# Retention opening in four steps of four heads by 256 tokens, in place of four chunks of eight heads by 128 tokens

## The chip, the cores and the metric

The kernel runs on one core of a Trainium2 chip. The core has a matrix engine (TensorE, "PE" in the profile, with its weight loads as "PEld"), VectorE (DVE), ScalarE (ACT), GpSimd (POOL) and SyncE (SP), which here only issues transfers. Each engine takes its own instructions in order and waits on semaphores for the others. Sixteen DMA engines move data between the chip's memory (HBM) and the on-chip SBUF; TensorE writes its results into PSUM, which has eight banks of 2 KB in each of 128 partitions. The metric is the device time of one execution in microseconds, the median of several.

## The reference

Two layers follow one another. The first is retention over q, k, v of 8 batches, 8 heads, 576 positions and 64 numbers each: causal attention without softmax, with a decay for each head. The second is a bilinear feed-forward network (FFN) over the 4608 tokens, 512 wide with 1536 features.

```python
scores = scale * np.matmul(q, k.transpose(0, 1, 3, 2))
gamma = 1.0 - 2.0 ** (-5.0 - np.arange(H))
rel = pos[:, None] - pos[None, :]
Dmat = np.where(rel >= 0, gamma[:, None, None] ** rel, 0.0)
attn_out = np.matmul(scores * Dmat, v)
x = attn_out.transpose(0, 2, 1, 3).reshape(B * S, H * D)
return ((x @ w_a) * (x @ w_b)) @ w_out
```

Since the decay is a power of the distance, `gamma**(s-t) = gamma**s * gamma**-t`. The kernel scales v by `gamma**-t` (the table `vs`), masks the plain scores, and scales the result by `scale * gamma**s` (the table `qs`). What keys of earlier chunks contribute is carried in a state, the sum of k^T v for each head.

## The kernel before

**The FFN** (`ffn_block`, L581 to L641) goes in blocks of 512 tokens (two of 256 after the first). A block forms `pa = x w_a` (L592) and `pb = x w_b` (L607) for each of 12 groups of 128 features, 4 matmuls each, casts pa on ACT (L600), multiplies on DVE (L612) and then forms `po` (L627), which leaves through `osb`. It reads x transposed, the tile `xT` of four chunks of 128 features. The first block takes its feature groups in runs of 3, 4 and 5, pa first and then pb (`WCOLS`, L579), since the weights arrive in these pieces.

**The retention** is woven into the FFN's instruction stream on PE, at places written by hand as PE cost (`todo`, L718 to L740). Most of it is done in pairs of 128-token chunks by `stretch`, with the PE array split into four quarters of 64x64 (`QUADS`). Only the first six chunks of 128 tokens are done one by one, and the first four of these form the opening: they have to be ready before the FFN can begin with its first 512 tokens.

**The opening** is the loop at L663 to L679. For a chunk i of 128 tokens with all 8 heads:
- `load(i)` (L116) brings q, k and v, 256 KB each, by SP (L121). A row of the transfer is one token of one head, 64 float32, 256 bytes.
- `cast(i)` (L241): q to bf16 on ACT (L250), k on DVE for chunks 0 and 3 (L252) and on POOL for chunks 1 and 2 (L254), v times `vs` on POOL (L255).
- `transposes(i)` (L262): four PE transposes for q and four for k (L269), each group into a PSUM tile `tp`; ACT copies q's out, DVE k's (L272).
- `scores(i)` (L307): eight matmuls `sc` of 64 rows (L316), one for each head, keys by queries; DVE masks them into `sT` in two instructions (L322).
- `state(i)` (L275): four matmuls `kv` (L287) add a chunk to the running sum in one PSUM bank that stays in place through the batch; ACT casts the diagonal blocks to the state (L304, L305).
- `outputs(i)` (L330): eight matmuls from the state (L341, none for chunk 0) and eight from the keys (L349) give `o`; DVE scales it by `qs` into xT (L356).

The program order of the loop sets each engine's queue. Before chunk i's state is cast, ACT has the q cast of chunk i+1 in front of it; `flush` puts the masks on DVE. The `warm` matmuls (L647) are products of the identity with itself, without use for the result; `idle` (L656) gives their number ahead of the scores and behind the state. The tiles `tp`, `kv2`, `w`, `pa`, `pb` and `po` share a ring of four PSUM banks (`ps_ffn`), `sc` has two banks, `kv` and `o` one each.

POOL also issues the weight transfers, which cast to bf16 on the way: `load_w(0, W1)` and `load_w(W1, W2)` ahead of the cast of chunk 3, the rest and `wo` after the loop. SP then waits with a small transfer (`gate`, L685) for the first of `wo` before it issues the loads of chunks 4, 5 and later pairs.

Ahead of the loop POOL makes index tables, the identity and the masks, ACT the tables `vs` (L184) and the first 640 columns of `qs` (L191); the remaining 128 columns of `qs` and the tables of the pairs (`pair_tables`, L198) are made during the first FFN block.

Of the kernel before, what the change touches and what calls it, by code (L numbers as in the profile page):

```python
# [10 lines left out]
FP32 = mybir.dt.float32  # L11
# [7 lines left out]
def kernel(  # L19
# [10 lines left out]
    nc = tc.nc  # L30
# [28 lines left out]
    def pool(name, bufs, space=None):  # L59
# [18 lines left out]
    opening = ExitStack()  # L78
    ps_open = opening.enter_context(
        tc.tile_pool(name="ps_open", bufs=1, space=PS))  # L80
    ps_o = {}
# [61 lines left out]
    for i in range(4):  # L143
        load(i)


    idxp_i = const.tile([128, PER], INT32)
    nc.gpsimd.iota(idxp_i[:, 0:MID + 1], pattern=[[128, MID + 1]], base=0,
                   channel_multiplier=1)
    nc.gpsimd.iota(idxp_i[:, MID + 1:PER], pattern=[[128, PER - MID - 1]],  # L150
                   base=64, channel_multiplier=1)
    idxv_i = const.tile([128, BL, 2], INT32)
    nc.gpsimd.iota(idxv_i, pattern=[[256, BL], [128, 2]], base=0,
                   channel_multiplier=1)
# [6 lines left out]
    make_identity(nc, identity)  # L161
    mask = const.tile([128, 128], BF16)
    nc.gpsimd.memset(mask, 1.0)
    nc.gpsimd.affine_select(
        out=mask, in_=mask, compare_op=ALU.is_ge, fill=0.0,
        base=0, pattern=[[1, 128]], channel_multiplier=-1)
    mask2 = const.tile([128, 128], BF16)
    nc.gpsimd.tensor_copy(mask2, mask)
    nc.gpsimd.memset(mask2[0:64, 64:128], 0.0)
    mask3 = const.tile([128, 64], BF16)  # L170

    lgp = const.tile([128, HP], FP32)
    for c in range(HP):
# [4 lines left out]
    idxp_f = const.tile([128, PER], FP32)  # L178
    nc.vector.tensor_copy(idxp_f, idxp_i)
    nc.vector.tensor_scalar_add(idxp_f[64:128, MID:MID + 1],  # L180
                                idxp_f[64:128, MID:MID + 1], -float(S))
    vs = const.tile([128, PER, H], FP32)
    for h in range(H):
        nc.scalar.activation(vs[:, :, h], idxp_f, AF.Exp,  # L184
                             bias=0.0, scale=-math.log(gammas[h]))
# [12 lines left out]
    def pair_tables(step):  # L198
# [12 lines left out]
        else:  # L211
            make_qs(step - 5, S + 64, S + 192)
# [4 lines left out]
    for t in states:  # L217
        nc.vector.memset(t, 0.0)
# [10 lines left out]
    natural, transposed, kv_of, state_of, scored = {}, {}, {}, {}, {}  # L229
    sums_of, states_of = {}, {}  # L230
# [6 lines left out]
    def flush():  # L237
        while later:
            later.pop(0)()

    def cast(i, on="pool"):  # L241
# [11 lines left out]
        else:  # L253
# [4 lines left out]
            vs[:, i % PER, :].unsqueeze(2).to_broadcast([128, H, D]),  # L258
# [16 lines left out]
    def state(i):  # L275
# [5 lines left out]
        if not kv_of:  # L281
            kv_of[0] = ps_open.tile([128, HP, 128], FP32, tag="kv",
# [500 lines left out]
```

## Time and profile before

| | us |
|---|---|
| median of 4 runs (336.4 to 338.75) | 336.59 |
| the profiled execution, device time | 336.15 |
| its span, first to last instruction | 334.4 |
| PE busy in it | 321.6 (96%) |
| DVE / ACT / POOL busy | 164.6 / 124.6 / 112.3 |
| first pa matmul of the FFN starts at | 21.24 |

The span is divided into 40 slices of 8.4 us in the profile's rows of digits; a 9 means that the engine was busy for 90% of the slice or more. In the timeline a row has start, length, engine, source line, operation, output and input tiles with shapes, and, in brackets, how long the engine had been idle and what ended that. In the chain of waits a row has start, length and the work that the end depended on. In the stages a row has the stretch in us, its length, then busy time and instruction count of PE, PEld, DVE, ACT and POOL, the granted clock, the DMA share (over 1 where packets of one engine overlap) and GB/s. A PE matmul is pipelined: the length in its row includes a latency of some 0.2 to 0.3 us, while the next one may start after 0.03 to 0.2 us.

### The profile page before, as it was taken

Reading aid. Unit: us, or ns where it says so; the run is one execution under the profiler, and the core shown is the slowest. Engines: PE = TensorE matmul, PEld = TensorE weight load, DVE = VectorE, ACT = ScalarE, POOL = GpSimd, SP = SyncE. Lnnn points to the kernel's source line nnn. Section 1 sums busy time; section 2 is a strip of 40 time slices with the busy share of each in tenths; the row PEclk is TensorE's granted clock in tenths of the full one; section 3 lists DMA queues with packets and bytes.
Section 4 is the critical chain, followed back from the end, with each engine's and each line's share of the span. In section 5 each row is a group of like instructions: output and inputs, shape, how many; then the busy total and the mean of one; then the engine's idle time right before and its main releaser. Section 6 shows DMA issues by size and latency. Waiting matters only on the chain.

```text
span 334.4 us, 8313 instructions
## 1 busy us (share of the span) xinstructions
PE 321.6 (96%) x3458; PEld 165.4 (49%) x3458; DVE 164.6 (49%) x307; ACT 124.6 (37%) x261; POOL 112.3 (34%) x139
## 2 busy tenths in 40 slices
PE   2989999999999999999999999999999999999995
PEld 1544445857744454545454545454545454444443
DVE  4646346465746465476237623762475347414321
ACT  8534433443624343353225322523352334213321
POOL 4670016961547448266143603370330000000000
PEclk9999999999999999999999999999999999999999
DMA  9999999999999999999599259964960420020002
GB/s 172 207 187 208 210 199 211 263 210 204 164 195 233 185 216 255 191 189 172 142 228 191 59 144 194 185 113 134 217 92 3 127 63 2 3 94 31 0 33 94
DMA packets 152230, 50.35 MB, mean 151 GB/s; under 512 B 142848, under 2 KB 147712, under 8 KB 152192
## 3 DMA queue, kind: packets, MB, share of 16 engines
q1 hardware_dynamic: 147440, 45.10, 70.2%
q0 software_dynamic: 4752, 4.72, 8.8%
q8 instruction: 27, 0.44, 0.6%
q14 instruction: 11, 0.09, 0.1%
HBM read 37.75 MB, written 9.44 MB: 141 GB/s over the span
## 4 chain that ended last, share of the span: by engine, by line
PE 93%; DVE 2%; DMA 2%; SPq 1%; ACT 1%; issue 0%; POOL 0%; ACTq 0%; DVEq 0%
PE pa L592 28%; PE pb L607 28%; PE po L627 28%; DMA kf<-in_k_dram 2%; PE o L525 2%; PE o L538 1%; PE sc L499 1%; PE kv L448 1%; PE w L651 1%; PE tp L269 1%; SPq L121 1%; DVE sT L322 1%; PE sc L316 1%; PE o L349 0%; PE o L341 0%
## 5 line engine op out<-in xcount | busy, mean ns | idle before, releaser
L612 DVE TENSOR_TENSOR hT<-ha,pb 128x512 bf16<-128x512 bf16 (+1 forms) x120 | 75.8, 633 | 98.3 <-PE pb L607 86.7
L592 PE MATMUL pa<-xT,wa_sb 128*128 128x512 bf16 (+1 forms) x480 | 111.5, 358 | 1.3 <-DVE xT L356 1.1
L600 ACT CAST ha<-pa 128x512 bf16<-128x512 f32 (+1 forms) x120 | 64.9, 542 | 126.5 <-PE pa L592 125.9
L607 PE MATMUL pb<-xT,wb_sb 128*128 128x512 bf16 (+1 forms) x480 | 111.4, 358 | 0.1
L627 PE MATMUL po<-wo_sb,hT 128*128 128x512 bf16 (+1 forms) x444 | 97.3, 373 | 0.0
L607 PEld LDWEIGHTS <-wb_sb 128*128 128x128 bf16 x480 | 46.9, 98 | 47.7 <-issue 1.1
L592 PEld LDWEIGHTS <-wa_sb 128*128 128x128 bf16 x480 | 45.9, 98 | 47.7 <-issue 2.4
L627 PEld LDWEIGHTS <-hT 128*128 128x128 bf16 x444 | 42.4, 98 | 47.0
L388 POOL CAST qkb<-qf 64x1024 bf16<-64x1024 f32 x15 | 15.4, 1029 | 81.5 <-DMA qf<-in_q_dram 68.9
L638 DVE COPY osb<-po 128x512 f32<-128x512 f32 (+1 forms) x18 | 12.2, 676 | 42.9 <-PE po L627 42.9
L393 POOL TENSOR_TENSOR vb<-vf,vs 128x1024 bf16<-128x1024 f32 x15 | 28.5, 1901 | 7.7 <-DMA vf<-in_v_dram 2.8
L636 ACT COPY osb<-po 128x512 f32<-128x512 f32 (+1 forms) x19 | 10.9, 574 | 49.0 <-PE po L627 49.0
L547 DVE TENSOR_TENSOR xT<-o,qs 128x512 bf16<-128x512 f32 x30 | 19.6, 681 | 5.5 <-PE o L538 5.5
L467 DVE TENSOR_TENSOR sums<-kv,sums 128x256 f32<-128x256 f32 x47 | 19.8, 422 | 4.6 <-PE kv L448 3.1
L508 DVE TENSOR_TENSOR sT<-sc,mask 128x512 bf16<-128x512 f32 x30 | 19.7, 679 | 0.0
L388 POOL CAST qkb<-kf 64x1024 bf16<-64x1024 f32 x15 | 15.5, 1033 | 9.5 <-DMA kf<-in_k_dram 9.0
L392 POOL CAST qkb<-qf 64x512 bf16<-64x512 f32 x30 | 17.6, 614 | 1.5 <-DMA qf<-in_q_dram 0.9
L392 POOL CAST qkb<-kf 64x512 bf16<-64x512 f32 x30 | 17.6, 614 | 0.9
L479 ACT CAST states<-sums 64x512 bf16<-64x512 f32 (+1 forms) x30 | 17.2, 574 | 0.5
L255 POOL TENSOR_TENSOR vb<-vf,vs 128x512 bf16<-128x512 f32 x6 | 6.3, 1047 | 29.7 <-DMA vf<-in_v_dram 27.1
L269 PE MATMUL tp<-identity,qkb 128*128 128x128 bf16 x48 | 5.4, 264 | 6.4 <-ACT qkb L250 5.8
L322 DVE TENSOR_TENSOR sT<-sc,mask 128x512 bf16<-128x512 f32 x12 | 7.7, 685 | 2.4 <-PE sc L316 2.4
(71 smaller groups left out, 142.1 us busy)
## 6 DMA issues: line engine op xcount, KB each, us to landing
out_dram<-osb SPq DMA_DIRECT2D x35, 256.0 KB, 2.3
qf<-in_q_dram SPq DMA_DIRECT2D x32, 256.0 KB, 4.5
kf<-in_k_dram SPq DMA_DIRECT2D x32, 256.0 KB, 5.4
vf<-in_v_dram SPq DMA_DIRECT2D x32, 256.0 KB, 5.1
wo_sb<-in_moe_w_out_dram POOLq DMA_DIRECT2D x3, 512.0 KB, 18.3
qf<-in_q_dram SPq DMA_DIRECT2D x8, 128.0 KB, 3.9
kf<-in_k_dram SPq DMA_DIRECT2D x8, 128.0 KB, 5.6
vf<-in_v_dram SPq DMA_DIRECT2D x8, 128.0 KB, 4.7
```

Of the source, the lines that this page charges most:

```text
L388: nc.gpsimd.tensor_copy(qkb[0:64, w], t[0:64])
L392: nc.gpsimd.tensor_copy(to[:, :, 1 - r], fro[:, :, r])
L393: nc.gpsimd.tensor_tensor(vb.rearrange("p (k h d) -> p k h d", k=2, h=H), vf.rearrange("p (k h d) -> p k h d", k=2, h=H), vs2[:, n % BL].u ...
L467: nc.vector.tensor_tensor(sums[:, i], own, prev, op=ALU.add)
L479: nc.scalar.copy(into[half(1 - r)].rearrange("p (k a) c d -> p a k (c d)", a=2)[:, 1, which.start // 2: which.stop // 2], sums[half(r)].re ...
L508: nc.vector.tensor_tensor(sT[:, on].rearrange("p c k s -> p (c k) s"), sc[:, on].rearrange("p c k s -> p (c k) s"), mask3.unsqueeze(1).to_ ...
L547: nc.vector.tensor_tensor(x_of(t0, 128).rearrange("p c (a s) -> p c a s", a=2), o[:, :, :, kp].rearrange("p a c s -> p c a s"), qs[:, :, s ...
L592: nc.tensor.matmul(pa[:, 0:n], wa_sb[:, c, fs], xT[:, c], start=(c == 0), stop=(c == NC - 1))
L600: nc.scalar.copy(ha[:, 0:n], pa[:, 0:n])
L607: nc.tensor.matmul(pb[:, 0:n], wb_sb[:, c, fs], xT[:, c], start=(c == 0), stop=(c == NC - 1))
L612: nc.vector.tensor_tensor(hT[:, F, 0:n], has[F][:, 0:n], pb[:, 0:n], op=ALU.mult)
L627: nc.tensor.matmul(po[:, 0:width], hT[:, F, u * 128:(u + 1) * 128], wo_sb[:, F, cols], start=(F == 0), stop=(F == NF - 1))
```

## The change

The opening works on the same first 512 tokens, all of them of batch 0, in another cut: a step is four heads of a pair of chunks, 256 tokens. `STEPS` lists (pair, half of the heads) as (0,0), (1,0), (0,1), (1,1).

- `load_step`: a partition holds two neighbouring tokens, so that a row of the transfer is two tokens of one head, 512 bytes. There are still twelve loads of 256 KB from SP.
- `cast_step`: q on ACT, k on DVE for steps 0 and 3, on POOL for 1 and 2; the copy puts even and odd tokens (`kp`) apart. v times `vs` is two POOL instructions, one for each kp.
- `transpose_step`: as before, four and four; ACT's copy of q weaves even and odd tokens back into order.
- `score_step`: 16 matmuls of 64 keys by 128 queries, on the array's four quarters. Chunk a of the pair is at partitions 64a to 64a+63. The mask `mask_s` takes the two parities into account.
- `state_step`: instead of a running sum in one bank, states are summed on PE from the chunks' keys and values each time, in a bank of the ring `ps_ffn`: one state behind the first chunk of the pair, one behind the second. That is 16 matmuls for pair 0 and 32 for pair 1, which adds pair 0 again. ACT converts each in two pieces of 64x128: the first state ahead of the next step's casts, the second behind them.
- `output_step`: two or four matmuls of 128x128 from states and 16 quarter matmuls from keys, into `o` of two banks; DVE scales it in two instructions of 256 columns, one for each pair of heads j.
- The pools `ps_step`, `ps_chunk` and `ps_pair` follow each other in the same two banks.
- The second weight issue is put behind the cast of step 3. The masks for later chunks and the index table `idxv_i` are made by POOL after all weight issues (`make_masks`), and ACT makes 512 columns of `qs` first and 256 later. The `warm` counts are the same.

```diff
+    def load_step(n, hh):
+        if n not in paired:
+            paired[n] = [stage.tile([128, 2 * DM], FP32, tag=name, name=name)
+                         for name in ("qf", "kf", "vf")]
+        for t, src in zip(paired[n], (q, k, v)):
+            nc.sync.dma_start(
+                t[:, hh * DM:(hh + 1) * DM]
+                .rearrange("p (h e) -> p h e", h=4),
+                src[0, 4 * hh:4 * hh + 4, 256 * n:256 * n + 256, :]
+                .rearrange("h (p two) d -> p h (two d)", two=2))
+    STEPS = [(0, 0), (1, 0), (0, 1), (1, 1)]
+    for s in STEPS:
+        load_step(*s)
...
+    def make_masks():
+        nc.gpsimd.iota(idxv_i, pattern=[[256, BL], [128, 2]], base=0,
+                       channel_multiplier=1)
+        nc.gpsimd.memset(mask, 1.0)
+        nc.gpsimd.affine_select(
+            out=mask, in_=mask, compare_op=ALU.is_ge, fill=0.0,
+            base=0, pattern=[[1, 128]], channel_multiplier=-1)
+        nc.gpsimd.tensor_copy(mask2, mask)
+        nc.gpsimd.memset(mask2[0:64, 64:128], 0.0)
...
-            make_qs(step - 5, S + 64, S + 192)
+            make_qs(step - 5, 512, S + 192)
...
+    def cast_step(i, on):
+        n, hh = STEPS[i]
+        qf, kf, vf = paired[n]
+        qkb = half_of(nat, i, [2, DM], BF16, "qkb")
+        vb = half_of(nat, i, [DM], BF16, "vb")
+        def given(t):
+            return t[:, hh * DM:(hh + 1) * DM].rearrange(
+                "p (h k d) -> p h k d", h=4, k=2)
+        def taken(t):
+            return t.rearrange("p (k h d) -> p h k d", h=4, k=2)
+        nc.scalar.copy(taken(qkb[:, 0]), given(qf))
+        if on == "dve":
+            nc.vector.tensor_copy(taken(qkb[:, 1]), given(kf))
+        else:
+            nc.gpsimd.tensor_copy(taken(qkb[:, 1]), given(kf))
+        for kp in (0, 1):
+            nc.gpsimd.tensor_tensor(
+                taken(vb)[:, :, kp], given(vf)[:, :, kp],
+                vs[:, 4 * hh:4 * hh + 4, 2 * n + kp].unsqueeze(2)
+                .to_broadcast([128, 4, D]), op=ALU.mult)
+        natural[n, hh] = (qkb, vb)
+        transposed[n, hh] = half_of(qkt_pool, i, [2, DM], BF16, "qkT")
+    def transpose_step(n, hh, w):
+        qkb, qkT = natural[n, hh][0], transposed[n, hh]
+        tp = ps_ffn.tile([128, 4, 128], BF16, tag="ab", name="tp")
+        for c in range(4):
+            nc.tensor.transpose(tp[:, c, :], qkb[:, w, c * 128:c * 128 + 128],
+                                identity)
+        if w == 0:
+            nc.scalar.copy(
+                qkT[:, 0].rearrange("p (j x k) -> p k j x", j=2, k=2),
+                tp.rearrange("p (k j) x -> p k j x", k=2))
+        else:
+            nc.vector.tensor_copy(qkT[:, 1], tp.rearrange("p c x -> p (c x)"))
+    def queries(n, hh, r, j, a):
+        c0 = j * 256 + a * 128
+        return transposed[n, hh][r, 0, c0:c0 + 128]
+    def score_step(n, hh):
+        qkT = transposed[n, hh]
+        sc = ps_sc.tile([128, 2, 2, 256], FP32, tag="sc", name="sc0")
+        for j in (0, 1):
+            for kp in (0, 1):
+                for r, a in QUADS:
+                    k0 = kp * 256 + j * 128 + a * 64
+                    nc.tensor.matmul(
+                        sc[half(a), r, j, kp * 128:kp * 128 + 128],
+                        qkT[half(r), 1, k0:k0 + 64],
+                        queries(n, hh, half(r), j, a),
+                        start=(j == 0 and kp == 0), stop=True,
+                        skip_group_check=True)
+        sT = st_pool.tile([128, 2, 2, 256], BF16, tag="sT", name="sT0")
+        scored[n, hh] = sT
+        def masked(r):
+            nc.vector.tensor_tensor(
+                sT[:, r], sc[:, r],
+                mask_s.rearrange("p k s -> p (k s)").unsqueeze(1)
+                .to_broadcast([128, 2, 256]), op=ALU.mult)
+        later.append(lambda: masked(0))
+        later.append(lambda: masked(1))
+    def state_step(n, hh):
+        kv = ps_ffn.tile([128, 2, 2, 64], FP32, tag="ab", name="kv0")
+        fresh = {0, 1}
+        for behind in (0, 1):
+            parts = [(0, slice(0, 128))] if n else []
+            parts.append((n, slice(0, 128) if behind else half(0)))
+            for m, rows in parts:
+                qkb, vb = natural[m, hh]
+                for j in (0, 1):
+                    for kp in (0, 1):
+                        for r in (0, 1):
+                            e0 = kp * 256 + (2 * j + r) * 64
+                            nc.tensor.matmul(
+                                kv[half(r), behind, j, :],
+                                qkb[rows, 1, e0:e0 + 64],
+                                vb[rows, e0:e0 + 64],
+                                start=r in fresh, stop=True,
+                                skip_group_check=True)
+                            fresh.discard(r)
+        def convert(behind):
+            to = state_after[n, behind][:, 2 * hh:2 * hh + 2]
+            for r in (0, 1):
+                nc.scalar.copy(to[half(r), :, half(r)], kv[half(r), behind])
+        return convert
+    def output_step(n, hh):
+        vb = natural[n, hh][1]
+        sT = scored.pop((n, hh))
+        o = ps_o[0].tile([128, 2, 512], FP32, tag="o", name="o0")
+        for a in (0, 1):
+            if (n, a) == (0, 0):
+                continue
+            st = state_after[n, 0] if a else state_after[n - 1, 1]
+            for j in (0, 1):
+                nc.tensor.matmul(o[:, a, 128 * j:128 * j + 128],
+                                 st[:, 2 * hh + j, :],
+                                 queries(n, hh, slice(0, 128), j, a),
+                                 start=(j == 0), stop=True,
+                                 skip_group_check=True)
+        for j in (0, 1):
+            for kp in (0, 1):
+                for a, r in QUADS:
+                    e0 = kp * 256 + (2 * j + r) * 64
+                    nc.tensor.matmul(
+                        o[half(r), a, 128 * j:128 * j + 128],
+                        vb[half(a), e0:e0 + 64],
+                        sT[half(a), r, j, kp * 128:kp * 128 + 128],
+                        start=((n, a, j, kp) == (0, 0, 0, 0)), stop=True,
+                        skip_group_check=True)
+        for j in (0, 1):
+            c = 2 * hh + j
+            nc.vector.tensor_tensor(
+                x_of(256 * n, 256)[:, c].rearrange("p (a s) -> p a s", a=2),
+                o[:, :, 128 * j:128 * j + 128],
+                qs[:, c, 256 * n:256 * n + 256]
+                .rearrange("p (a s) -> p a s", a=2), op=ALU.mult)
...
+    make_qs(0, 0, 512)
+    make_qs(1, 0, 512)
+    cast_step(0, "dve")
+    for w in (0, 1):
+        transpose_step(*STEPS[0], w)
+    make_qs(2, 0, 512)
+    make_qs(3, 0, 512)
+    for i, s in enumerate(STEPS):
         if idle[i][0]:
             warm(idle[i][0])
-        scores(i)
+        score_step(*s)
+        convert = state_step(*s)
         flush()
+        convert(0)
         if i == 2:
             load_w(0, W1)
+        if i < 3:
+            cast_step(i + 1, "dve" if i == 2 else "pool")
+        if i == 2:
             load_w(W1, W2)
-        if i < 3:
-            cast(i + 1, "dve" if i == 2 else "act")
-        state(i)
+        convert(1)
         if idle[i][1]:
             warm(idle[i][1])
         if i < 3:
-            transposes(i + 1)
-            outputs(i)
-            flush()
+            for w in (0, 1):
+                transpose_step(*STEPS[i + 1], w)
+        output_step(*s)
     load_w(W2, DFF)
     for i in (0, 1, 2):
         load_wo(i)
-    outputs(3, halves=True)
-    flush()
+    make_masks()
+    ps_next("ps_chunk")
     nc.sync.dma_start(gate, wo_sb[0:1, 3, 0:64])
```

## The prediction

> **What bounds the kernel now.** First the page, for the engine that sets the end.
>
> ```profile
> span 334.4 us, 8313 instructions
> ...
> PE 321.6 (96%) x3458; PEld 165.4 (49%) x3458; DVE 164.6 (49%) x307; ACT 124.6 (37%) x261; POOL 112.3 (34%) x139
> ...
> PE   2989999999999999999999999999999999999995
> ```
>
> The reader is to see that TensorE (PE) is full in every slice after the third. The change touches what stands before that. The timeline puts the first FFN product (pa) at 21.24 us; its first four matmuls, one feature block, take 4 x 0.216 and leave PE free at 22.10. From there the instruction lists of the two kernels agree on PE but for a few waits, so whatever the opening wins or loses moves the end by as much, if PE stays fed. The second view is the chain of waits, restricted to 8 to 22 us.
>
> ```profile
> 3.65 5.09 DMA kf<-in_k_dram
> ...
> 8.80 0.62 POOL qkb L254
> ...
> 11.74 1.28 PE w L651 x3
> 13.02 0.85 PE tp L269 x8
> ...
> 14.54 0.54 PE w L651 x2
> 15.08 0.35 PE sc L316 x8
> ...
> 15.46 1.29 DVE sT L322 x2
> 16.75 0.55 DVE qkb L252
> ...
> 18.31 0.32 PE w L651
> 18.63 0.33 PE sc L316 x8
> ...
> 20.77 0.43 DVE xT L356
> ```
>
> A transfer stands on this chain only up to 8.74 us. After that PE, DVE and their handoffs carry it: warm-up matmuls, transposes, scores, mask, the DVE cast of the last k. Third, the stages: DMA is saturated through the opening, yet that is not what the chain rests on.
>
> ```profile
> 4.00:8.00 4.00, 2.08 (x20) 1.46 (x20) 1.37 (x3) 3.27 (x5) 1.04 (x1) 1.00 1.34 218
> 8.00:12.00 4.00, 3.30 (x32) 2.02 (x31) 2.46 (x6) 2.76 (x7) 1.65 (x2) 1.00 1.35 218
> 12.00:16.00 4.00, 4.00 (x43) 2.40 (x42) 2.28 (x5) 1.88 (x5) 2.98 (x4) 1.00 1.34 217
> ```
>
> Fourth, two timeline rows that show PE at half and at full pace: the same eight score matmuls.
>
> ```profile
> 10.59 0.61 PE L316 MATMUL sc<-qkT 64*128 64x128 bf16 x8
> ...
> 15.02 0.40 PE L316 MATMUL sc<-qkT 64*128 64x128 bf16 x8
> ```
>
> Starts of a 128-column matmul are 0.107 us apart until 14.07 us, 0.056 after.
>
> **The loads.** Twelve loads of 256 KB, as before, in 512 rows of 512 bytes and not 1024 of 256. Before, 10352 packets in 12 us on 16 engines are 18.5 ns a packet, 1.21 us a load; loads ended at 5.15 us (first k), 8.8, 11.2, 12.4, 13.6, the last v near 17.2. A 512-byte row is not in the trace. From above it costs two small ones (37 ns, no gain); from below one (18.5 ns, 0.60 us a load). The nearest row is the weight transfer, which casts: 825 packets in 4 us, 77.6 ns for 2048 bytes read; 669 in 4 us, 95.7 ns for 2560. The slope is 0.035 ns a byte with 5 ns fixed: 23 ns for 512 bytes, 0.75 us a load, or 0.88 if the 4 ns by which a 256-byte packet exceeds this line remain. I take 0.80. The Trainium skill ("DMA: Bandwidth & Descriptors", Specifications and Why small descriptors are slow) puts the line rate at 512 bytes and more, and charges 3 fixed cycles on 8 for 256 bytes: 19 cycles for 22, 1.04 us a load. By my row the loads end 12 x 0.41 = 4.9 us earlier, by the page's cycles 2.0; the sum below is the same for both, as it waits for neither. At 1.21 the first v holds the first states for 0.4 us and the sum grows by about 0.3.
>
> **POOL.** Each v product is two of 256 columns. From 1047 ns for 512 and 1901 for 1024, 256 take 0.62, so 1.24 a step for 1.05. With v of the third step at 9.9 us, the first weights are issued at 11.2 (before 14.61) and land some 5.4 us later as before, 16.6. That buys nothing alone: they landed at 20.0 for a start at 21.24. Only two of the four issues now stand ahead of the last v product (12.9 to 14.1, before 17.8 to 18.9), which had slack. The masks for later chunks (about 1.1 us by the rows of their old place) and one index table move behind seven more DMA issues, to about 19.5. DVE's cast of that table gets a wait there; it comes at 26.4, so 7 us cover it. If they were gone, DVE's products behind it, and then PE, would wait.
>
> **PE.** A step has 16 scores of 64x64 (8 before), 16 or 32 state matmuls (4), 2 or 4 from states and 16 from keys (16). The 32 quarter-array matmuls of the pair stage take 0.45 us, 0.19 of it latency: 8 ns each, four side by side. With 128 columns, four per 0.056 (cold 0.107): scores cost what they did. States run in column pairs of 64: 8 or 16 pairs at 0.032 warm, 0.053 cold, 0.25 to 0.9 us for 0.22 to 0.43. The Trainium skill ("TensorEngine Tiling (Array Packing)", Key Properties) says that a change of tiling mode drains the array, which speaks against the change; the trace prices it: four matmuls of 0.109 from 65.09 end at 65.53, the quarters begin at 65.62, 0.09 us. A step changes mode some three times, half of it new; without the rule the sum is 0.4 us lower.
>
> **ACT and the new wait.** A step converts states in four pieces of 64x128: from 585 ns for 512 columns and 372 for 256, 0.26, with issue 0.28 each, so 1.1 for 0.75. Two of them are now put ahead of the next q cast. The tile is waited for whole, so ACT stands until all state matmuls of this step are done; behind it queue the q cast, then the copy of its transposes, and PE waits for both. Before, the q cast went first, and waited for its load alone.
>
> **The sum**, from step to step, with handoffs from the rows (q cast end to transpose copy 0.70 cold, 0.48 warm; scores to mask 0.73 and 0.44; two masks 1.29):
> - Step 0: shorter tables (2 x 0.1) let the q cast run at 4.33; transposes 4.98, scores 6.6, masks 7.3, states end 7.9 (v product 6.35), first conversions to 8.5.
> - Step 1: q cast 8.46 to 9.06 (before 8.11), transposes 9.12, scores 10.73 (10.59), masks 11.65 (11.35). 32 cold state matmuls end at 12.6, conversions 12.65 to 13.2.
> - Step 2: q cast 13.17 to 13.77 (before 11.17, but its transposes waited for warm-ups until 12.81), transposes 13.85, copies to 15.03, outputs to 15.0, two warm-ups, scores 15.62 (15.02), masks 16.06 to 17.35 (15.46 to 16.75).
> - Step 3: k cast on DVE 17.26 to 17.88, transposes to 18.15, two state matmuls and 16 keys to 18.6 (0.1 less than before), scores 19.05 (18.56), masks 19.49 to 20.78 (19.00 to 20.29), keys, first half of x at 21.7.
> - FFN: chunks 0 and 1 of x have been there since step 1, so the first two matmuls of pa run during the last scaling, 0.43 us ahead; the other two follow at 21.75 and 22.07, PE free at 22.29 for 22.10.
>
> So +0.2 us: 334.4 becomes 334.6 in span, 336.15 becomes 336.35, and the median 336.59, which lies 0.44 above its profiled execution, 336.8. The remaining edits are covered: four exponentials of 256 columns for 128 in the first FFN block (0.11 each, ACT busy at most 3.3 of 5 us there; 0.4 us uncovered), half the packets of SP's 12 issues, DVE's two scalings of 256 columns (0.42 each, pipelined, 0.76 for 0.69).
>
> **Rivals.**
> 1. *Loads were the pace.* For it: 217 GB/s from 2 to 16 us, ACT idle 1.9 us for q. If the steps follow the loads at 3.0 us instead of 3.6, the FFN begins 1.8 to 2.4 us sooner (its weights allow 16.6): 334.4. At the full 2.4 us pitch 332. Against: no transfer on the chain after 8.74, and my sum's pitch is ACT's and PE's own.
> 2. *Slower: the PE clock rises later.* The rows change from 0.107 to 0.056 at 14.07. The Trainium skill ("TensorE: Matmul & The Clock Gate", Part 1) gives a free-running window of 3.41 us that must be busy; the one that counted is then 10.66 to 14.07. In the new order PE is filled there by narrow state matmuls and a 0.02 to 0.2 us gap. If that does not count, the next chance is 17.48: second-step transposes, outputs, warm-ups and scores stay cold, masks start at 17.6 for 16.06, the end +1.7 us: 338.3. It decides from the point where that window misses. A longer ACT wait adds to it.
> 3. *The rows bring no speed* (37 ns each): 337.1, hidden but for the first states.
>
> **Numbers.** Likeliest, a tie within 1.2 us, 0.5: 336.8, own range 335.5 to 338.0. Rival 1: 0.19. Rival 2: 0.25. Rival 3: 0.06. One can tell about 0.5% (1.7 us) from no change here. Faster 0.19 from rival 1; slower 0.25 of rival 2 and its like, though 338.3 lies at the edge, plus 0.02 of the tie's tail; same 0.54. The range leaves out the far half of rivals 1 and 2: 334.4 to 338.8.
>
> **What would show it.** Loads landing 0.75 to 0.9 us apart; q cast of step 2 waiting for PE's states until 13.2; scores of step 2 near 15.6, the clock step at 14.1; first pa before the last two scalings, its fourth matmul near 22.1; from there 312.3 us to the end. The forecast is wrong if the q casts run as soon as their loads land, if the 0.107 starts last beyond 14.1, or if PE waits for weights or chunk 4 after the start.

## The result and the profile after

The changed kernel takes 337.96 us (median of 42 runs, 337.27 to 339.3) against 336.64 us for the kernel before on the same chips (61 runs, 336.02 to 338.75): a ratio of 1.0035, with a 95% interval of 1.0026 to 1.0043. It is 1.3 us slower, a little less than the 1.7 us that the prediction called the bound of a tie. The profiled execution took 339.06 us, 1.1 us more than its median, with a span of 337.3 us; that of before took 336.15 us, slightly below its median. So the two profiles differ by 2.9 us where the medians differ by 1.3, and the account of terms below is one of the profiles.

The page of the kernel after:

```profile
span 337.3 us, 8595 instructions
...
PE 324.2 (96%) x3590; PEld 167.6 (50%) x3590; DVE 165.5 (49%) x310; ACT 126.6 (38%) x269; POOL 114.4 (34%) x147
...
PE   2899999999999999999999999999999999999995
```

PE is full from the third slice on, as before. Almost the whole loss stands ahead of that: the fifth pa matmul, the one that needs a second block of weights and that the prediction used as its mark, starts at 24.54 us for 22.10. From there to the end it is 312.8 us for 312.3; most of this difference stands at 54.6 us, where transposes for the next chunk wait for DVE's cast of k.

The chain of waits of the kernel after, from 8 to 24.5 us (start, length, work):

```profile
8.03 0.74 PE kv L365 x13
...
8.79 0.26 ACT step_states L376
...
9.06 0.26 ACT step_states L376
...
9.35 0.63 ACT qkb L297
...
10.02 1.03 PE tp L314 x8
...
12.26 1.28 PE kv L365 x30
13.54 1.39 PE w L811 x3
14.93 0.91 PE tp L314 x8
...
17.33 0.35 PE sc L334 x16
...
18.64 0.63 ACT qkb L297
...
21.07 0.86 PE kv L365 x32
21.93 0.97 PE w L811 x4
```

No transfer and no POOL work is on it after 8.03 us. The pieces that the chain of before did not have are the state matmuls (kv), their conversions on ACT (step_states) and the q cast behind these (qkb): the order that the change put on ACT. The waits of ACT between 4 and 24 us say it in one line (line waited for: us in total, times, longest):

```profile
ACT step_states L376 <- PE kv L365: 6.4, 4, 2.2
```

The stages of the kernel after (stretch, length, busy time and count of PE, PEld, DVE, ACT, POOL, granted clock, DMA share, GB/s):

```profile
4.00:8.00 4.00, 1.94 (x26) 1.40 (x27) 1.56 (x4) 3.12 (x5) 1.20 (x2) 1.00 1.02 278
8.00:12.00 4.00, 2.71 (x56) 2.31 (x55) 1.04 (x3) 2.39 (x6) 2.42 (x4) 1.00 1.17 291
12.00:16.00 4.00, 4.00 (x59) 2.58 (x51) 2.03 (x5) 2.20 (x6) 3.82 (x6) 1.00 0.63 93
```

The transfers run at 291 GB/s for 218, and are over in the third stage. PE stands idle for 1.3 of 4 us in the second, for 0.7 before. The clock column says 1.00 although the starts of matmuls in the first three stages are those of the half clock. The trace's own record of the granted clock begins with its step to the full clock, at 16.63 us, for 14.06 us before; the column has 1.00 for all that lies ahead of the record. Two timeline rows of the kernel after show it: eight transposes ahead of the step and 16 scores behind it.

```profile
14.81 1.03 PE L314 MATMUL tp<-identity,qkb 128*128 128x128 bf16 x8
...
17.27 0.42 PE L334 MATMUL sc<-qkT 64*64 64x128 bf16 x16
```

### The profile page after: what moved, and what is told of

Its sections match the earlier page's. It is cut to its first block, busy times and chain, and to the rows that moved or that the text cites. A ratio compares the mean times of both kernels' runs of the same rounds, so it can differ in the third digit from the quotient of the medians.

```text
span 337.3 us, 8595 instructions
## 1 busy us (share of the span) xinstructions
PE 324.2 (96%) x3590; PEld 167.6 (50%) x3590; DVE 165.5 (49%) x310; ACT 126.6 (38%) x269; POOL 114.4 (34%) x147
## 4 chain that ended last, share of the span: by engine, by line
PE 93%; DVE 2%; ACT 1%; DMA 1%; issue 1%; POOL 0%; SPq 0%; ACTq 0%; POOLq 0%; DVEq 0%
PE pa L752 28%; PE pb L767 28%; PE po L787 27%; PE o L686 2%; PE sc L660 1%; PE o L699 1%; DMA vf<-in_v_dram 1%; PE kv L609 1%; PE kv L365 1%; PE w L811 1%; PE tp L314 1%; PE o L397 1%; DVE xT L526 0%; ACT qkb L297 0%; POOL vb L303 0%
## 5 line engine op out<-in xcount | busy, mean ns | idle before, releaser
L669 DVE TENSOR_TENSOR sT<-sc,mask 128x512 bf16<-128x512 f32 x30 | 19.8, 681 | 0.0
L425 POOL TENSOR_TENSOR vb<-vf,vs 128x512 bf16<-128x512 f32 x2 | 2.3, 1160 | 24.2 <-DMA vf<-in_v_dram 24.2
L314 PE MATMUL tp<-identity,qkb 128*128 128x128 bf16 x32 | 3.7, 288 | 6.5 <-ACT qkb L297 6.5
L686 PEld LDWEIGHTS <-states 64*64 64x64 bf16 x432 | 5.0, 108 | 6.1 <-issue 6.1
```

What stands on the lines that cost most here:

```text
L669: nc.vector.tensor_tensor(sT[:, on].rearrange("p c k s -> p (c k) s"), sc[:, on].rearrange("p c k s -> p (c k) s"), mask3.unsqueeze(1).to_ ...
```

## The experiments

Each time is followed by its ratio to the kernel before, timed beside it. Two theories stood against each other at first. The first: *the clock*. The step came 2.6 us late, because the new opening doesn't fill PE, and it is this that costs the time. The second: *the order on ACT*. The q cast queues behind the conversions, and PE starves. A third was *the work itself* (more state matmuls), and a fourth *the loads* (rows of 512 bytes that bring too little). The instants of the profiled executions are gathered here. The column of the sum has what the prediction worked out; "masks" is the start of DVE's first mask of a step.

| | clock step | first v landed | q cast 1 | masks 1 | masks 2 | masks 3 | fifth pa |
|---|---|---|---|---|---|---|---|
| the sum | 14.07 | 5.1 | 8.46 | 11.65 | 16.06 | 19.49 | 22.29 |
| before | 14.06 | 6.33 | 8.11 | 11.35 | 15.46 | 19.00 | 22.10 |
| after | 16.63 | 6.61 | 9.35 | 12.63 | 17.73 | 21.19 | 24.54 |
| cast first (1) | 14.36 | 6.05 | 7.75 | 11.02 | 15.90 | 19.24 | 22.59 |
| no pair 0 (2) | 15.90 | 6.61 | 9.35 | 12.64 | 17.02 | 20.48 | 23.33 |
| early warm-up (3) | 7.23 | 6.11 | 8.83 | 11.37 | 15.48 | 18.94 | 22.29 |
| 256-byte rows (4) | 14.21 | 6.58 | 9.31 | 12.60 | 16.90 | 20.66 | 24.01 |
| no last warm-ups (6) | 13.99 | 6.25 | 8.98 | 12.27 | 16.57 | 20.04 | 23.11 |
| where PE is idle (9) | 6.05 | 6.68 | 7.75 | 11.08 | 14.23 | 18.26 | 21.35 |

**1. The q cast first.** The kernel after, with ACT's first conversions put behind the next step's casts, as before.

```diff
         flush()
-        convert(0)
...
             cast_step(i + 1, "dve" if i == 2 else "pool")
+        convert(0)
         if i == 2:
             load_w(W1, W2)
         convert(1)
```

> The changed kernel with one move: ACT takes the q cast of the next step ahead of the conversion of the first state, as the kernel before did. If ACT's order is what costs (the q casts of steps 1 to 3 stood behind the conversions at 9.35, 14.13 and 18.64 us), scores of step 1 come near 10.7 instead of 11.6, those of step 2 near 16, and the time falls by about 1 us, to 337.0 (1.001 of before). If the late clock or the amount of PE work is what costs, the q cast is early and PE's later starts stay where they were: 337.8 to 338.0.

Measured: 337.38 us (14 runs, 336.02 to 338.99), 1.0012 times before [0.9991, 1.0033]. That is 0.6 us less than the kernel after, at the edge of what can be told. The q casts of steps 1 and 2 ran at 7.75 and 9.96 for 9.35 and 14.13. The masks of step 2 gained less, 1.83 us, since the chain of this kernel has PE and DVE where ACT stood.

```profile
8.41 1.03 PE tp L314 x8
...
12.06 1.39 PE w L811 x3
...
15.90 1.29 DVE sT L344 x2
17.19 0.35 DVE qkb L299
...
19.97 0.97 PE w L811 x4
```

The q that comes 4 us earlier in step 2 waits for the warm-ups on PE. The fifth pa of this profile is 1.96 us earlier than after's, but so are its clock step (14.36 for 16.63) and its first v (6.05 for 6.61); what the order alone is worth cannot be read from it, and the medians say some tenths.

**2. Without the first pair's share in the states.**

```diff
-            parts = [(0, slice(0, 128))] if n else []
+            parts = []
```

> The changed kernel without the 16 state matmuls of pair 0 in each step of pair 1; states behind pair 1 lack pair 0's part, so this part of the computation is left out. If the sums on PE cost by their own length, steps 1 and 3 lose half of 1.35 and 0.93 us of state matmuls: conversions of step 1 end 0.6 us earlier, the FFN starts 0.9 to 1.0 us earlier: 337.0. If they lie beside other work, 337.8 to 338.0.

Measured: 338.28 us (22 runs, 337.52 to 340.07), 1.0043 [1.003, 1.0057], above both expectations. Sixteen state matmuls fewer in each of two steps, and the median gained nothing. The opening of the profile did gain: behind shorter states the q cast of step 2 ran at 13.43 for 14.13, while neither kernel had the full clock, and the fifth pa stands at 23.33 for 24.54. Yet the execution took 339.23 us. From the fifth pa on it needed 1.4 us more than the kernel after, nearly all of it in one gap of PE, for which the profile shows no cause and which after does not have:

```profile
90.84 0.27 PE L752 MATMUL pa<-xT,wa_sb 128*128 128x256 bf16 x1 [1.15 <-issue]
```

Whether the other runs had this gap is not known. So the work itself is on the path of the opening; why the median shows nothing of that stays open.

**3. The clock early.** Five warm-up matmuls ahead of the first transposes, two between scores and states of step 0, three behind the states, places where PE waited for other engines.

```diff
-    idle = {0: (0, 0), 1: (0, 3), 2: (2, 4), 3: (1, 4)}
+    idle = {0: (0, 3), 1: (0, 3), 2: (2, 4), 3: (1, 4)}
...
+    warm(5)
     for w in (0, 1):
         transpose_step(*STEPS[0], w)
...
         score_step(*s)
+        if i == 0:
+            warm(2)
```

> The changed kernel with more warm-up matmuls where PE was idle: five ahead of the first transposes, two between scores and states of step 0, three behind those states. If the late rise of the PE clock (16.6 us in the profile) costs, it now rises by 10 us, the transposes, outputs and warm-ups up to 16.6 run at full pace, and the time falls by 1.0 to 1.8 us, to 336.2 to 337.0, with less scatter between runs (337.3 to 339.3 now). If the clock is not what costs, the warm-ups change nothing or delay step 1 by some 0.3: 337.9 to 338.3.

Measured: 336.63 us (14 runs, 336.22 to 337.61), 0.9996 [0.9981, 1.0012]. This takes back all of the 1.3 us. The chain of this kernel, from 8 us:

```profile
11.22 0.88 PE kv L365 x32
...
13.35 0.62 PE tp L314 x8
...
15.08 0.35 PE sc L334 x16
...
18.46 0.35 PE sc L334 x16
...
19.67 0.97 PE w L811 x4
```

The states of step 1 take 0.88 us for 1.28, the transposes of step 2 0.62 for 0.91, and these scores stand at 15.08 for 17.33 us. ACT's order is untouched. So an early clock is enough to win the loss back. This does not show that the late step alone was the loss: the clock came 7 us earlier here than in the kernel before, and in experiment 6, whose profile has the step at 13.99 as before, the fifth pa still stands 1.0 us later than before's. That it stands at 22.29 here, the very instant of the sum, is chance: the early clock makes up for other terms that the sum had too small, told below.

**4. Rows of 256 bytes in the new steps.** A load brings 128 tokens of all heads, as before; the steps then compute with wrong tokens, in the same shapes.

```diff
-                .rearrange("p (h e) -> p h e", h=4),
-                src[0, 4 * hh:4 * hh + 4, 256 * n:256 * n + 256, :]
-                .rearrange("h (p two) d -> p h (two d)", two=2))
+                .rearrange("p (h e) -> p h e", h=8),
+                src[0, :, 128 * (2 * n + hh):128 * (2 * n + hh) + 128, :]
+                .rearrange("h p d -> p h d"))
```

> The changed kernel with loads of 256-byte rows again: each of the twelve takes eight heads of 128 tokens, and the steps work on them as if they were four heads of 256, so that the values are not the reference's while all sizes and the order stay. If the rows bring time to the end, a load comes each 1.2 us instead of 0.9, the last v lands near 17.2 instead of 14.7, first weights are issued near 15 instead of 13.3, and the time rises by 0.5 us or more. If the opening waits for engines, not for loads, it stays within 0.4 us of 337.96; the first v landed at 6.33 with these rows before and at 6.61 after, so step 0 may even come 0.2 us sooner.

Measured: 338.69 us (14 runs, 337.82 to 339.44), 1.0046 [1.0029, 1.0063], 0.7 us more than the kernel after. The loads landed 1.2 us apart for 0.90, the last v at 17.98 for 14.69; the first v came no later (6.58 for 6.61). In its profile the fifth pa was not later than after's (there the clock had stepped at 14.21), but at 54.7 us transposes waited 0.85 us for DVE's cast of k, for 0.21 in after. So the longer rows are a gain, but a small one in this order.

**5. The kernel before, with the same early warm-up.**

```diff
-    idle = {0: (0, 0), 1: (0, 3), 2: (2, 4), 3: (1, 4)}
+    idle = {0: (0, 2), 1: (0, 3), 2: (2, 4), 3: (1, 4)}
...
+    warm(5)
...
+        if i == 0:
+            warm(1)
```

> The kernel before with the same kind of early warm-ups: five ahead of its first transposes, one between scores and states of chunk 0, two behind those states. If the clock's rise is what scatters the kernel before too (about one run in six near 338.4, the others near 336.5), the runs near 338.4 go away and the rest stay near 336.4, because its opening waits for loads (1.2 us each) where PE is slow: 336.2 to 336.6. Then the change, given the same clock (336.63), brings nothing. If the early clock is worth to the kernel before what it was worth to the changed one (1.3 us), the median falls to 335.3 and the change's own cost is 1.3 us whatever the clock does.

Measured: 336.54 us (22 runs, 336.38 to 338.13), 0.9987 [0.9976, 0.9998]. The clock stepped at 11.04 us, three microseconds earlier than before, and the median gained 0.1 to 0.3 us. Its chain shows why (8 to 23 us):

```profile
8.65 5.17 DMA vf<-in_v_dram
...
13.89 1.04 POOL vb L255
14.93 0.87 POOL wa_sb L221
15.80 0.76 POOL wb_sb L222
16.56 0.74 POOL wa_sb L221
17.30 0.75 POOL wb_sb L222
18.05 1.08 POOL vb L255
...
19.17 0.38 PE kv L287 x4
```

The kernel before has a second path to the same end: the loads of 256-byte rows, then POOL's product for chunk 2, four weight issues and the product for chunk 3, then the last states. It ends together with the path over PE that the prediction read: in the kernel before, the product for chunk 3 ends at 18.86 and the last states begin at 18.91.

```profile
17.78 1.08 POOL L255 TENSOR_TENSOR vb<-vf,vs 128x512 bf16<-128x512 f32 x1
...
18.91 0.38 PE L287 MATMUL kv<-vb,qkb 128*128 128x128 bf16 x4
```

An earlier clock only uncovers this path. The change removed it (the last product of v ends at 16.22, 4.8 us ahead of the last states), by its faster rows and by the place of the second weight issue; nothing of that could be seen in the time while the PE path was the longer one.

What did shrink is the scatter: of 75 runs of the kernel before beside it, 17 lie at 338.2 to 338.9, of these 22 only one above 337.3. That those are executions with a late clock step fits, but no profile caught one; a gap like that of experiment 2 would lengthen a run nearly as much.

**6. The kernel after without the last four warm-ups**, identical to it up to the states of step 3.

```diff
-    idle = {0: (0, 0), 1: (0, 3), 2: (2, 4), 3: (1, 4)}
+    idle = {0: (0, 0), 1: (0, 3), 2: (2, 4), 3: (1, 0)}
```

> The changed kernel without the four warm-ups behind the states of step 3. In its profile they stand between states and outputs there (21.86 to 22.7 us) while the masks end at 22.47, so without them the outputs start 0.55 us earlier: 337.4 (1.0019 of before). If the conversion of the first state (ends 22.5) is what the outputs wait for, 337.6 to 337.9.

Measured: 337.94 us (22 runs, 337.14 to 339.71), 1.002 [1.0007, 1.0033]: no change against the kernel after, where 337.4, or 337.6 to 337.9, was expected. In its profile the way from the masks of step 3 to the fifth pa is 3.07 us for 3.35, so that the four warm-ups did hold PE for 0.3 us. This profile is worth more than the time, as it caught an execution (337.42 us) in which the clock stepped at 13.99. These two rows of its timeline answer to those of after above:

```profile
14.45 0.62 PE L314 MATMUL tp<-identity,qkb 128*128 128x128 bf16 x8
...
16.10 0.42 PE L334 MATMUL sc<-qkT 64*64 64x128 bf16 x16
```

The same instructions in the same order stand 0.36 us earlier at the masks of step 1, when neither had the full clock (the first v had landed 0.36 us earlier), and 1.15 us earlier at those of step 3. The difference of 0.8 us is the clock's.

**7. Experiments 1 and 3 together.**

```diff
-    idle = {0: (0, 0), 1: (0, 3), 2: (2, 4), 3: (1, 4)}
+    idle = {0: (0, 3), 1: (0, 3), 2: (2, 4), 3: (1, 4)}
...
+    warm(5)
...
+        if i == 0:
+            warm(2)
...
-        convert(0)
...
+        convert(0)
...
         convert(1)
```

> Early warm-ups and the q cast ahead of the conversion together. If ACT's order costs apart from the clock, it gives here what it gives at best alone: in the profile with early warm-ups the chain of 8 to 17 us is conversion, q cast, transposes three times, and with the cast first it becomes masks and the k cast: 0.5 to 1.0 us less than 336.63, 335.6 to 336.1. If the clock was everything, 336.6.

Measured: 336.48 us (22 runs, 335.12 to 337.47), 0.9978 [0.9965, 0.9991]. By the medians the order on ACT is worth 0.15 us more, which cannot be told from nothing. The clock was not early in all its runs: in its profile, the longest of them, the early warm-ups missed and the clock stepped at 12.25. So this is no clean test of the order; experiment 11 comes nearer to one.

**8. Experiment 7 with warm-ups in step 0 alone**, to see what the later ones cost.

```diff
-    idle = {0: (0, 3), 1: (0, 3), 2: (2, 4), 3: (1, 4)}
+    idle = {0: (0, 3), 1: (0, 0), 2: (0, 0), 3: (0, 0)}
```

> The same without the warm-ups of steps 1 to 3 (three, two, four, one, four). If the clock stays up on the work itself, the chain loses up to 0.3 + 0.5 + 0.3 + 0.9 us of them and the FFN may start at 18.5 to 19.5, which its first weights (landed at 18.1) allow: 334.0 to 335.3, below both kernels. If the clock falls back in the gaps, or the chain goes over ACT and DVE beside them, 335.6 to 336.6.

Measured: 337.59 us (22 runs, 335.82 to 338.85), 1.0009 [0.9993, 1.0024], 1.1 us more than experiment 7 and above both expectations. In its profile the clock, up at 7.75 us, went down again at 17.99 and up at 24.81. The stretches of 3.41 us ahead of the fall and ahead of the second rise:

```profile
14.58:17.99 3.41, 1.61 (x46) 1.09 (x46) 2.80 (x5) 1.77 (x5) 3.40 (x6) 1.00 1.01 119
...
21.40:24.81 3.41, 3.41 (x10) 1.22 (x8) 0.27 (x1) 0.97 (x2) 1.58 (x8) 0.50 1.24 207
```

The masks of step 2 had come to stand at 14.29 and the first pa at 20.79, 2.6 us earlier than after; but the first nine or ten matmuls of the FFN then started 0.43 us apart. Each run's mean granted clock tells how common this is: 17 of the 22 have 0.988 to 0.990, about what the 6.8 us at half clock take off in a run of 336, and a median of 337.65 us; five have 1.000 and a median of 336.29. So the warm-ups have a use: they hold the clock, and its fall costs 1.4 us here.

**9. Warm-ups where PE is idle.** Experiment 7, with one after the first transposes, none behind the states of step 1, seven behind those of step 2, where PE waits for DVE's cast of k, and two in step 3.

```diff
-    idle = {0: (0, 3), 1: (0, 3), 2: (2, 4), 3: (1, 4)}
+    idle = {0: (0, 3), 1: (0, 0), 2: (0, 7), 3: (0, 2)}
...
     warm(5)
     for w in (0, 1):
         transpose_step(*STEPS[0], w)
+    warm(1)
```

> The changed kernel with the q cast first, early warm-ups (five, one, two, three in step 0) and later warm-ups only where PE waits for ACT and DVE anyway: none in step 1, seven behind the states of step 2, two behind those of step 3, none ahead of scores. If the order and the clock are the two costs, the clock is up by 10 us and stays up, masks of step 2 start near 14.3 as without warm-ups, the FFN at 19 to 20 and the time is 334.5 to 335.6, below both kernels. If the clock needs the warm-ups that were on the path, it falls again near 18 us and the time is 336.5 or more.

Measured: 335.22 us (6 runs, 334.87 to 335.76), 0.9929 [0.9901, 0.9957]: it beats both kernels, 2.7 us below the kernel after. The clock rose at 6.05 us and stayed. Its chain, from 7 us:

```profile
8.10 0.54 PE kv L365 x14
...
9.77 0.75 ACT qkT L317
...
12.99 0.74 ACT qkT L317
...
14.23 1.29 DVE sT L344 x2
15.52 1.04 DVE qkb L299
...
17.52 0.42 PE sc L334 x16
...
20.21 1.94 PE pa L752 x7
```

Here the clock, the cast order and the rows of 512 bytes act together; the rest is ACT's copy and DVE's mask and cast.

**10. The kernel before, with warm-ups placed in the same way**; the edit is against experiment 5.

```diff
-    idle = {0: (0, 2), 1: (0, 3), 2: (2, 4), 3: (1, 4)}
+    idle = {0: (0, 2), 1: (0, 3), 2: (0, 4), 3: (0, 2)}
...
+    warm(1)
```

> The kernel before with the same treatment: warm-ups early (five, one, one, two), none ahead of scores, four and two where PE waits in steps 2 and 3. Its loads end near 17.2 us and its first weights land at 20, so with the clock up it can gain only what its warm-ups had on the path (0.2 to 0.5 us): 336.0 to 336.5. If it gains as much as the changed kernel does from this, the new layout has no part in that gain.

Measured: 336.34 us (12 runs, 335.8 to 337.4), 0.9971 [0.995, 0.9991]. Beside experiment 9, on the same chip, the new steps are 1.1 us faster than the old ones if both are kept warm. In the change as it was made this gain is hidden: an early clock alone brought it to 336.63, and it took the cast order and the placing of the warm-ups as well to come to 335.22.

**11. Experiment 9 with the old place of the first conversions**, ahead of the q cast as in the change.

```diff
         flush()
+        convert(0)
...
-        convert(0)
...
         convert(1)
```

> The 335.2 us version with the one move of ACT's order undone: the first conversion ahead of the q cast again, clock and warm-ups as there. If the order has a price of its own with the clock up, q casts of steps 2 and 3 come at 12.2 and 15.5 instead of 10.4 and 13.6 and the time rises by 0.4 to 1.0 us, to 335.6 to 336.2. If the order only mattered while PE was slow, 335.2.

Measured: 336.98 us (14 runs, 335.85 to 338.55), 0.9994 [0.9977, 1.0012], 1.8 us more than experiment 9 and above both expectations. In its profile the clock, up at 6.63, was down from 13.46 to 16.87. The two windows of this kernel up to there:

```profile
10.05:13.46 3.41, 1.91 (x70) 1.55 (x69) 2.37 (x5) 1.98 (x5) 2.44 (x5) 1.00 1.06 260
13.46:16.87 3.41, 3.41 (x62) 2.58 (x60) 2.09 (x5) 1.67 (x6) 3.40 (x6) 0.50 0.79 87
```

Not every run had such a fall, and the mean granted clock tells them apart. Seven have 0.993 to 0.995, about what one window of 3.41 us at half clock takes off, and a median of 337.19 us; the other seven have 0.999 or 1.000 and a median of 336.10. So the order costs by the wait itself, 0.9 us against experiment 9 (these seven lie from 335.85 to 337.05, its six runs from 334.87 to 335.76), and in half of the runs by another 1.1 us, as it leaves PE idle for so long that the clock falls. The runs are few, on another chip than experiment 9's, and when the clock rose in each is not on record.

**12. Experiment 9 with rows of 256 bytes**, the edit of experiment 4 (wrong tokens in the same shapes).

```diff
-                .rearrange("p (h e) -> p h e", h=4),
-                src[0, 4 * hh:4 * hh + 4, 256 * n:256 * n + 256, :]
-                .rearrange("h (p two) d -> p h (two d)", two=2))
+                .rearrange("p (h e) -> p h e", h=8),
+                src[0, :, 128 * (2 * n + hh):128 * (2 * n + hh) + 128, :]
+                .rearrange("h p d -> p h d"))
```

> The 335.2 us version with 256-byte rows: each load takes eight heads of 128 tokens and the steps work on them as if they were four heads of 256, so that the values are not the reference's while sizes and order stay. With the clock up and the order mended the steps no longer hide the loads: q and k of the fourth step land near 15 and 16.2 instead of 12.9 and 13.8, first weights near 20.5 instead of 18.7, and the time rises by 0.8 to 1.5 us, to 336.0 to 336.7, about the kernel before under the same warm-ups (336.34). If loads are still hidden, 335.3 to 335.6.

Measured: 337.14 us (22 runs, 336.1 to 338.51), 1.0009 [0.9997, 1.0022], 1.9 us more than experiment 9 (0.7 us between experiment 4 and the kernel after), and above both expectations. Now a transfer is on the chain:

```profile
9.63 6.63 DMA qf<-in_q_dram
...
16.28 0.62 ACT qkb L297
```

So the loads do become the pace, once PE and ACT no longer are. The last q landed at 16.26, 1.4 us later than the spacing of the others asks, so that not all of the 1.9 us need be the rows' own. The trace has one packet of 16 KB, of the DMA queue called instruction, in the midst of this load, from 13.54 to 14.86 us; in the kernel before it starts at 16.41, as the packets of the loads end. That it held up the load fits, but is not shown: with such a packet at 13.85, the q of experiment 4 landed in time (14.97) and only the k behind it late.

## Why the prediction was right, and where it was not

The forecast, a tie at 336.8 us, held: 337.96 is in the likeliest case's own range, at its upper end, and within 0.5%. That it held is in good part luck. The sum asked for 0.2 us more than before, the change costs 1.3, and the price of rival 2 (338.3) lies nearer to the result than the forecast does. One of the prediction's own signs of being wrong came true as well: starts 0.107 us apart were not to last beyond 14.1, and in the profile they lasted to 16.63. Three steps of its sum were off. Against it the fifth pa of the profile, one of the longest executions, is 2.25 us late, and this divides as follows.

- **The loads, +0.9.** The sum took the first v at 5.1 us and said that it waits for no load. It landed at 6.61, no earlier than with the old rows (6.33 before), and since ACT's q cast of step 1 now queues behind the states made from it, it sets the whole chain: 9.35 for 8.46. Half of this step was seen ("at 1.21 the first v holds the first states"), and priced at 0.3. The rate was near the estimate: 2344 packets in 4 us from 8 to 12 are 27.3 ns each, loads 0.90 us apart, for 0.80 taken from the weight rows; its own second reading of them, 0.88, was nearer, and the estimate from the cycle count after the Trainium skill ("DMA: Bandwidth & Descriptors", Why small descriptors are slow), 1.04, is about as far off on the other side. But the first loads came slower than this rate, 1.8 us from the first k to the first v. Why they do stays open (it landed between 6.05 and 6.73 us in the profiles with rows of 512 bytes, between 6.33 and 6.58 in those with 256).
- **The clock, +0.8.** The sum took the step at 14.07, as in the trace of before. This is rival 2, which named the mechanism (the window that has to be busy is filled by narrow state matmuls and a gap) and the sign, and was given a price of 1.7 us on one missed window at 17.48. The windows of the kernel after up to its step show the miss:

```profile
9.81:13.22 3.41, 3.20 (x70) 2.71 (x72) 1.68 (x4) 1.41 (x4) 2.43 (x5) 1.00 1.08 268
13.22:16.63 3.41, 3.41 (x44) 2.06 (x39) 1.12 (x3) 2.38 (x6) 3.40 (x6) 1.00 0.58 52
```

  The step that failed is to have read an instant off one execution as a property of the kernel. What the kernel sets is from when on PE is filled; the windows lie differently in each execution, so that by their length of 3.41 us the step can come as much later than it could. It stood at 13.99 and at 16.63 for the same instructions (experiment 6 and after). With the clock early (experiment 3) the median goes to 336.63.
- **The last states, +0.55.** The 32 matmuls of step 3 were put at 0.5 us: 16 pairs of 0.032. The pairs kept this pace: within a group the trace has them at 21.54, 21.57, 21.60. But a state is summed from parts in two tilings, 128x64 and 64x64, and at each change the next pair stands 0.12 us on for 0.03. The 0.09 us that the prediction read for a change of mode is right; its term for the states had none of them. From the first state matmul to the start of the next work it is 0.86 us, 21.00 to 21.86. The four warm-ups behind then hold PE until 22.73, when masks and conversions had ended at 22.47 and 22.50, and the outputs from the states come behind the masks instead of ahead of them. So 0.36 us of this are the states' own length; the hold of the warm-ups, 0.3 us by the profile of experiment 6, covers the rest.

Experiment 6 checks this division. With the clock step where the sum had it (13.99), its fifth pa is 0.8 us behind the sum: 0.5 for the first v at 6.25, 0.3 for the last states.

What held: the scores in 64x64 quarters cost what they did (0.42 us warm and 0.64 cold, for 0.40 and 0.61). A conversion takes 259 ns, POOL's two products of v 1.20 us together. The weights were early (first landed at 18.53, later than the 16.6 worked out and still 4.9 us ahead of their use). ACT's wait for the states is there, 6.4 us of it. Two matmuls of pa run ahead of the others, during the last scaling. ACT's weaving copy was overlooked in the sum: 0.73 us for the 0.58 of a plain one.

*Rival 1*, the loads as the pace, did not come about, and the reason given against it ("no transfer on the chain after 8.74") was too narrow. A chain shows one path, and experiment 5 shows a second path, over the loads and POOL, that ended with it. The prediction had read this path's last product of v (17.8 to 18.9) and said that it had slack; the slack was 0.05 us. Removing the path bought nothing until PE's was shortened as well; then the new steps were worth 1.1 us (experiment 9 against 10), and their rows alone, by experiment 12, up to 1.9. *Rival 3*, 37 ns a row, fell: 27.3.

What stays open: how the 1.3 us of the medians divide, as against the terms of the profile; the slow first loads; the late q of experiment 12; and the gap of experiment 2, with how often it falls into a run.

## What to carry to other kernels

An opening that ends in a full TensorE is timed by when its clock rises as well as by its chain: look in the trace's record for that instant, take it as one draw out of a window, and ask whether the change keeps PE filled before it. Warm-ups belong where PE waits anyway, and in the right number: too few later on lost 1.1 us here (experiment 8 against 7), and their placing, with one more of them early, won 1.3 (9 against 7). A profile shows one run; the mean granted clock of each told here which runs had lost it. Where a change removes a path that is not on the chain, it gains nothing until the chain's own path is shortened; test the two together before dropping either.

## What the runs showed of the hardware

- *Changes of the clock come in whole windows, and a half-empty one is enough to lose it.* In experiment 8 the clock fell 10.24 us after it rose and rose again 6.83 us later, in experiment 11 after 6.83 and 3.41: 3, 2, 2 and 1 times the 3.41 us that the Trainium skill gives ("TensorE: Matmul & The Clock Gate", Part 1). Its rule for losing the clock (HAM oscillation), a gap of more than some 3.4 us, is too lenient here: it fell after windows in which the profile has PE busy for 1.61 and 1.91 of 3.41 us, and was kept with 2.37 and 2.38 (experiments 10 and 12). Runs with such a fall were 1.4 us longer in experiment 8 (two windows at half clock) and 1.1 us in experiment 11 (one).
- *Busy time, as the profile gives it with the latency of each matmul, is not what counts for the rise.* A window with 3.20 us of 70 matmuls of 64 or 128 columns did not raise the clock (after), nor did 3.19 in experiment 1, while 2.89 us with three warm-ups of 512 columns did (experiments 3 and 8). With two of these, 2.81 us did not (experiment 5). What is counted was not found.
- *A change between matmul tilings costs about 0.09 us*: in the state sums of after, where 128x64 and 64x64 alternate, the next start comes after 0.12 us for 0.03.
- *A 512-byte row costs 27.3 ns a packet for 18.5 of a 256-byte one*, 291 for 218 GB/s.
